# The first stage of a Fourier-mixing and gated-feed-forward kernel in another order

## The chip, the cores and the metric

The kernel runs on one core of a Trainium2 chip. A core has five engines that work side by side, each with its own queue of instructions taken strictly in order: TensorE (matrix products; PE in the profile, its weight loads PEld), VectorE (DVE), ScalarE (ACT), GpSimd (POOL) and SyncE (SP, which here issues the transfers between main memory and the on-chip SBUF). Matrix products land in PSUM, in a few banks that are used in turn. The metric is the time of one execution on the device in microseconds (us), lower is better.

## The reference

For x of 2048 rows and 448 columns, float32 throughout:

```
xn = (x - mean) / sqrt(var + 1e-5)                      # per row
a, b = xn @ hid_re.T, xn @ hid_im.T                     # 448 x 448
s  = seq_re @ a - seq_im @ b                            # 2048 x 2048
g  = silu((gelu(xn @ w_gate) * (xn @ w_up)) @ w_down)   # 448 -> 1792 -> 448
out = x + s * g
```

## The kernel before, in words

**Precision.** To keep float32 accuracy, each operand is split in two: a high part, rounded by a copy to the type `float32r` (mostly on ScalarE), and a low part, the difference of the value and its high part (a subtraction, mostly on VectorE). A product is then three matmuls: high x high, high x low, low x high. In the code these are "hh", "hl" and "lh"; the last, narrow block of the inner dimension goes in "last".

**Tiles.** Rows are dealt in four chunks (`c` = 0 to 3) of four times 128 rows. `xr[c]` holds the raw and then the normalised rows, `xth[c]` and `xtl[c]` the high and low part of the turned (transposed) rows, `xf[c]` a full-precision copy of the first two turned blocks. The inner width 1792 of the feed-forward part is dealt in 14 blocks `f`, in groups of two. For group 0 the two products of gate and up are made plainly (`gu_mm`, `first`, `gateup`); from group 1 on they are made with Strassen's combinations (`strassen`), which take sums and differences of the `xf` blocks of two chunks. `combine(p)` makes these four subtractions for the pair of chunks p, and returns a function that splits one combination into high (`th`) and low (`tl`) part.

**Statistics.** `stats(c, k0, n)` returns four functions: `one(i)` takes mean and variance of 128 rows (two VectorE instructions, L95 and L96), `root` the square root on ScalarE and two short VectorE instructions (L100 to L102), `newton` the reciprocal with a refining step (L106 to L110), `norm(i)` writes the normalised rows (L118). `turn_mm` turns 128 rows on TensorE (four transposes, L127, into one of two PSUM tiles), `turn_split` copies the high part and `xf` on ScalarE (L132, L133) and subtracts the low part on VectorE (L134).

**Weights.** `load_w` brings a block of gate and up weights into one of two `raw` buffers, taken in turn; `prep_w` returns `high` (a copy of 1024 columns, L177 on ScalarE or L179 on VectorE) and `low` (L182 for 768 columns, L184 for 256 columns of half the partitions). `load_d` and `prep_d` do the same for the down weights `wd` (L227 high, L228 low). A `raw` buffer is loaded again when the subtraction that reads it is through.

**Feed-forward.** `act` makes the Gelu of the gate product on ScalarE (L261) and returns `m` (product with the up half, L264, VectorE), `h` (high part, L265, ScalarE) and `l` (low part, L266, VectorE). `down` multiplies them with `wd`: per 128 rows six matmuls into `po` (L286), then a copy into the accumulator `gacc` (L293 on ScalarE for group 0). Between these steps `down` calls what it is handed in `between`.

**Order.** The whole order is written out by hand: under `tc.manual_schedule()` each engine's queue is the order in which the Python code calls it. SyncE issues in the order of the `load_` calls, and transfers share the DMA engines. What an engine waits for follows from the data and from tiles that are used again. The stage at issue is the first: loading, statistics and turning of the four chunks beside group 0 (L378 to L563). In it `first` works on chunk 0 in two halves of 256 columns (rows 0 and 1 of the chunk, then 2 and 3), and later chunks are prepared beside the products of earlier ones. The rest, six groups of Strassen products (L575 to L661), the hidden transform (L683) and the sequence transform (L742 to L764), is the longest part of the time and stays as it is.

Of the kernel before, what the change touches and what calls it, by code (L numbers as in the profile page):

```python
# [8 lines left out]
F32 = mybir.dt.float32  # L9
# [17 lines left out]
GROUPS = [(f, f + 1) for f in range(0, NF, 2)]  # L27
# [3 lines left out]
def fnet_geglu(ctx: ExitStack, tc: tile.TileContext, x, ct, et, wgu, wd, out):  # L31
# [13 lines left out]
    nc = tc.nc  # L45
# [40 lines left out]
    def load_x(c, k0, k1):  # L86
        nc.sync.dma_start(xr[c][:, k0:k1], xv[:, 4 * c + k0 : 4 * c + k1])

    def stats(c, k0, n):
        st = const.tile([P, 4, 6], F32, name=f"st{c}_{k0}", tag="st", bufs=2)  # L90
        mv = const.tile([P, 4, 2], F32, name=f"mv{c}_{k0}", tag="mv", bufs=3)
        sd = const.tile([P, 4, 4], F32, name=f"sd{c}_{k0}", tag="sd", bufs=3)

        def one(i):
            nc.vector.bn_stats(st[:, i], xr[c][:, k0 + i, :D])  # L95
            nc.vector.bn_aggr(mv[:, i], st[:, i])  # L96

        def root():
            r, t, w = sd[:, :n, 0], sd[:, :n, 1], sd[:, :n, 2]
            nc.scalar.activation(t, mv[:, :n, 1], AF.Sqrt, bias=epst)  # L100
            nc.vector.tensor_scalar(w, mv[:, :n, 1], EPS, -0.5, op0=ALU.add, op1=ALU.mult)
            nc.vector.tensor_scalar_mul(sd[:, :n, 3], mv[:, :n, 0], -1.0)  # L102

        def newton():
            r, t, w = sd[:, :n, 0], sd[:, :n, 1], sd[:, :n, 2]
            nc.vector.reciprocal(r, t)  # L106

            nc.vector.tensor_mul(t, r, r)
            nc.vector.tensor_mul(t, t, w)
            nc.vector.scalar_tensor_tensor(r, t, 1.5, r, op0=ALU.add, op1=ALU.mult)  # L110

        def norm(i, eng=nc.vector):
            v = xr[c][:, k0 + i]
            if eng is nc.scalar:
                eng.activation(v, v, AF.Identity, bias=sd[:, i, 3:4])
                eng.activation(v, v, AF.Copy, scale=sd[:, i, 0:1])
            else:
                eng.tensor_scalar(  # L118
                    v, v, mv[:, i, 0:1], sd[:, i, 0:1], op0=ALU.subtract, op1=ALU.mult
                )  # L120

        return one, root, newton, norm
# [7 lines left out]
    def turn_split(c, k, pt):  # L130
        sl = slice(k * P, (k + 1) * P)
        nc.scalar.activation(xth[c][:, :, sl], pt, AF.Copy)  # L132
        nc.scalar.activation(xf[c][:, :, sl], pt[:, :2], AF.Copy)  # L133
        nc.vector.tensor_sub(xtl[c][:, :, sl], pt, xth[c][:, :, sl])  # L134
# [30 lines left out]
    def load_w(f):  # L165
        raw = raw_tile()
        nc.sync.dma_start(raw[:, :1024], wgu[f].rearrange("p b f -> p (b f)"))
        return raw

    def prep_w(slot, raw):  # L170

        w = a_w[:, 2560 * slot : 2560 * slot + 1792]
        wh, wl = w[:, :1024], w[:, 1024:]

        def high(copy):
            if copy is None:
                nc.scalar.activation(wh, raw[:, :1024], AF.Copy)  # L177
            else:
                copy(wh, raw[:, :1024])  # L179

        def low():
            nc.vector.tensor_sub(wl, raw[:, 256:1024], wh[:, 256:])  # L182

            nc.vector.tensor_sub(wh[64:, :256], raw[64:, :256], wh[64:, :256])  # L184

        return high, low, (wh, wl)

# [33 lines left out]
        )  # L221
        return rv

    def prep_d(grp, rv, sub=None):
        o = 1792 * (grp[0] // 2 % 2)
        w = a_d[:, o : o + 1792].rearrange("p (a f d) -> p a f d", a=2, f=2)
        nc.scalar.activation(w[:, 0], rv, AF.Copy)  # L227
        (sub or nc.vector.tensor_sub)(w[:, 1], rv, w[:, 0])  # L228
        return w

    def gu_mm(ps, w, g, c, cols, late_xtl=False):
        hs, ls = zip(*[block(w, k, g) for k in range(4)])
        hh = [(hs[k], xth[c], k) for k in range(3)]
        hl = [(hs[k], xtl[c], k) for k in range(3)]
        lh = [(ls[k], xth[c], k) for k in range(3)]
        last = [(hs[3], xth[c], 3), (hs[3], xtl[c], 3)]
        mm = hh + lh + last[:1] + hl + last[1:] if late_xtl else hh + hl + lh + last
        for n, (a, xt, k) in enumerate(mm):
            nc.tensor.matmul(ps[:, cols], a, xt[:, k, cols], start=n == 0, stop=n == len(mm) - 1)  # L239
# [8 lines left out]
    def hs_tile(name, dt=FR):  # L248
        return sb.tile([P, 2, 512], dt, name=name, tag="hs", bufs=6)
# [7 lines left out]
    def act(f, c, pg):  # L257
        acts[0] += 1
        gt = tmp(acts[0] % 2)
        hs = new_hs(f, c)  # L260
        nc.scalar.activation(gt, pg[0], AF.Gelu_apprx_tanh)  # L261

        return (
            lambda: nc.vector.tensor_mul(gt, gt, pg[1]),  # L264
            lambda: nc.scalar.activation(hs[:, 0], gt, AF.Copy),  # L265
            lambda: nc.vector.tensor_sub(hs[:, 1], gt, hs[:, 0]),  # L266
        )
# [109 lines left out]
    with tc.manual_schedule():  # L377
        load_x(0, 0, 1)  # L378
        load_x(0, 1, 2)
        load_x(0, 2, 4)  # L380
        w_raw = [load_w(0), load_w(1)]
        load_x(1, 0, 4)
        load_x(2, 0, 4)
        load_x(3, 0, 4)
# [50 lines left out]
        xl = [xtl[0][:, :, k * P : (k + 1) * P] for k in range(4)]  # L435
        nc.scalar.activation(xh[0], t0[2], AF.Copy)
        nc.scalar.activation(xh[1], t1[2], AF.Copy)
        one, root, newton, norm = stats(0, 2, 2)
        one(0)
        one(1)  # L440
        ws = [prep_w(i, w_raw[i]) for i in range(2)]
        ws[0][0](nc.vector.tensor_copy)
        nc.vector.tensor_sub(xl[0], t0[2], xh[0])
        nc.vector.tensor_sub(xl[1], t1[2], xh[1])
        root()
        ws[1][0](None)
        for k, t in enumerate((t0, t1)):
            nc.scalar.activation(xf[0][:, :, k * P : (k + 1) * P], t[2][:, :2], AF.Copy)
        ws[0][1]()
        newton()  # L450
        norm(0)
        norm(1)
        ws[1][1]()
        ws = [w[2] for w in ws]
        draw = load_d(GROUPS[0])
        first(0, half[0], ("hh", "hl", "lh", "last"))
# [5 lines left out]
        one(1)  # L462
        turn_split(*t2)
        turn_split(*t3)
        wdn = prep_d(GROUPS[0], draw, nc.gpsimd.tensor_sub)
        one(2)
        one(3)
        root()
# [8 lines left out]
        turn_split(*t0)  # L477
        turn_split(*t1)
        one, root, newton, norm = stats(2, 0, 4)
        one(0)  # L480
        one(1)
        s_raw = load_w(GROUPS[1][0])
        pg = gu_ps(0, 1)
        gu_mm(pg[0], ws[0], 0, 1, half[0], True)
# [1 line left out]
        gu_mm(pg[1], ws[0], 1, 1, half[0])  # L486
        turn_split(*t2)
        turn_split(*t3)
        m0, h0, l0 = act(0, 0, pgs[0])
        m1, h1, l1 = act(1, 0, pgs[1])  # L490
        m0()
        h0()
        l0()
        gu_mm(pg[0], ws[0], 0, 1, half[1], True)
        gu_mm(pg[1], ws[0], 1, 1, half[1])
        m1()
        h1()
        m0, h0, l0 = act(0, 1, pg)
        one(2)
        l1()  # L500
        one(3)
        root()
        m0()
        h0()
        newton()
        for i in range(4):
            norm(i)
        l0()
        pg = gu_ps(1, 1)
        for g in range(2):  # L510
            gu_mm(pg[g], ws[1], g, 1, slice(0, 512))
        one, root, newton, norm = stats(3, 0, 4)
        one(0)
        one(1)
        xf[2] = hs_tile("xf2", F32)
        turn_split(*turn_mm(2, 0))
        down(0, 0, wdn, [lambda k=k: turn_split(*turn_mm(2, k)) for k in (1, 2, 3)])
        m1, h1, l1 = act(1, 1, pg)
        one(2)
        m1()  # L520
        h1()
        one(3)
        l1()
        root()
        newton()
        norm(0)
        norm(1)
# [4 lines left out]
        for c in (2, 3):  # L532
            if c == 2:
                draw = load_d(GROUPS[1])
            else:
                s_raw2 = load_w(GROUPS[1][1])
            m0, h0, l0 = gateup(0, c, ws[0])
            between, between1 = [lambda: (m0(), h0()), l0], []
            if c == 2:
                xf[3] = hs_tile("xf3", F32)  # L540
                turn = lambda k: turn_split(*turn_mm(3, k))
                between = [
                    lambda: (m0(), h0(), norm(2)),
                    lambda: (l0(), norm(3), turn(0)),
                    lambda: turn(1),
                    lambda: turn(2),
                ]
                between1 = [lambda: turn(3)]
            down(0, c - 1, wdn, between)
            if c == 2:  # L550
                nws[0] = prep_s(2, s_raw, nc.vector)
            else:
                one = combine(0)
                for i in range(4):
                    one(i)
                nwdn = prep_d(GROUPS[1], draw)
                late_split = combine(1)
            m1, h1, l1 = gateup(1, c, ws[1], between1)
            m1()
            if c == 2:  # L560
                h1()
                l1()
        late = (h1, l1)  # L563


# [241 lines left out]
```

## Time and profile before

| | before |
|---|---|
| median of 3 runs | 813.77 us (813.35 to 815.39) |
| profiled execution | 814.51 us, of it 812.7 us from the first to the last instruction |
| mean granted TensorE clock | 0.997 |
| TensorE busy | 801.8 us, 99% |
| TensorE weight loads busy | 715.0 us, 88% |
| VectorE busy | 415.0 us, 51% |
| ScalarE busy | 238.7 us, 29% |
| GpSimd busy | 54.4 us, 7% |

The busy times are sums over the execution. VectorE's share differs by stage: it is 7 to 8 tenths in the first third of the span and 2 to 3 tenths in the last part. Matmuls are pipelined, so that the time of one matmul (some 390 ns) is longer than the distance from one to the next. A line number stands for the code line that made the instruction; "issue" stands for time in which an engine waited for nothing that the profile shows.

### The profile page before, as it was taken

Reading aid. Unit: us, or ns where it says so; the run is one execution under the profiler, and the core shown is the slowest. Engines: PE = TensorE matmul, PEld = TensorE weight load, DVE = VectorE, ACT = ScalarE, POOL = GpSimd, SP = SyncE. Lnnn points to the kernel's source line nnn. Section 1 sums busy time; section 2 is a strip of 40 time slices with the busy share of each in tenths; the row PEclk is TensorE's granted clock in tenths of the full one; section 3 lists DMA queues with packets and bytes.
Section 4 is the critical chain, followed back from the end, with each engine's and each line's share of the span. In section 5 each row is a group of like instructions: output and inputs, shape, how many; then the busy total and the mean of one; then the engine's idle time right before and its main releaser. Section 6 shows DMA issues by size and latency. Waiting matters only on the chain.

```text
span 812.7 us, 9386 instructions
## 1 busy us (share of the span) xinstructions
PE 801.8 (99%) x3868; PEld 715.0 (88%) x3868; DVE 415.0 (51%) x626; ACT 238.7 (29%) x356; POOL 54.4 (7%) x62
## 2 busy tenths in 40 slices
PE   8899999999999999999999999999999999999997
PEld 7788888888888888888889999999999999999997
DVE  8776786766776676776763233232232222223221
ACT  3574432322322232232221224122222222222220
POOL 0000120010010010000000000111111111111110
PEclk9999999999999999999999999999999999999999
DMA  8001010000010110100020012344444333444441
GB/s 307 24 0 52 24 52 23 27 27 23 27 49 1 33 43 1 49 23 24 23 77 1 1 38 77 103 140 133 132 127 126 127 127 127 126 127 127 127 127 60
DMA packets 19372, 58.09 MB, mean 71 GB/s; under 512 B 2048, under 2 KB 8064, under 8 KB 18944
## 3 DMA queue, kind: packets, MB, share of 16 engines
q1 hardware_dynamic: 19328, 57.48, 22.1%
q8 instruction: 30, 0.49, 0.2%
q14 instruction: 14, 0.11, 0.0%
HBM read 53.81 MB, written 3.67 MB: 71 GB/s over the span
## 4 chain that ended last, share of the span: by engine, by line
PE 95%; DVE 3%; ACT 1%; issue 1%; DMA 0%; DVEq 0%
PE x L306 22%; PE po L286 16%; PE py L758 13%; PE py L757 13%; PE py L756 13%; PE ab L683 9%; PE x L314 5%; PE gu L239 2%; PE gu L417 1%; PE pt L127 1%; DVE st L95 1%; DVE xr L118 0%; DVE tmp L264 0%; DMA xr<-x 0%; DVE tl L83 0%
## 5 line engine op out<-in xcount | busy, mean ns | idle before, releaser
L286 PE MATMUL po<-wd,hs 128*128 128x448 f32 x672 | 153.0, 366 | 0.0
L286 PEld LDWEIGHTS po<-wd,hs 128*128 128x128 f32 x672 | 125.8, 188 | 14.6 <-ACT gacc L293 0.2
L306 PE MATMUL x<-xt,w 128*128 128x512 f32 x504 | 135.0, 391 | 0.0
L306 PEld LDWEIGHTS x<-xt,w 128*128 128x128 f32 x504 | 94.6, 188 | 17.0
L758 PE MATMUL py<-xt,w 128*128 128x448 f32 x256 | 93.5, 365 | 0.0
L756 PE MATMUL py<-xt,w 128*128 128x448 f32 x256 | 93.5, 365 | 0.0
L757 PE MATMUL py<-xt,w 128*128 128x448 f32 x256 | 93.5, 365 | 0.0
L295 DVE TENSOR_TENSOR gacc<-gacc,po 128x448 f32<-128x448 f32 x96 | 59.3, 618 | 60.8 <-PE po L286 60.8
L306 PE MATMUL x<-th,w 128*128 128x512 f32 x192 | 71.4, 392 | 1.0 <-DVE tmp L264 1.0
L756 PE MATMUL py<-ab,c 128*128 128x448 f32 x192 | 70.1, 365 | 0.0
L757 PE MATMUL py<-ab,c 128*128 128x448 f32 x192 | 70.1, 365 | 0.0
L758 PE MATMUL py<-ab,c 128*128 128x448 f32 x192 | 70.1, 365 | 0.0
L683 PE MATMUL ab<-w,xt 128*128 128x448 f32 x256 | 68.0, 365 | 0.0
L83 DVE TENSOR_TENSOR w<-raw,w 128x1024 fp32r<-128x1024 f32 (+1 forms) x23 | 27.8, 1210 | 73.1 <-ACT w L82 73.1
L82 ACT ACTIVATE w<-raw 128x1024 fp32r<-128x1024 f32 (+1 forms) x23 | 24.2, 1050 | 128.4 <-DMA raw<-ct 118.2
L763 POOL TENSOR_TENSOR gacc<-gacc,s 128x448 f32<-128x448 f32 x15 | 31.0, 2067 | 429.3 <-DVE gacc L762 429.3
L314 PE MATMUL x<-xt,w 128*128 128x512 f32 x192 | 59.2, 389 | 0.0
L762 DVE TENSOR_TENSOR gacc<-gacc,py 128x448 f32<-128x448 f32 (+1 forms) x17 | 10.1, 593 | 87.5 <-PE py L758 87.5
L683 PEld LDWEIGHTS ab<-w,xt 128*128 128x128 f32 x256 | 48.1, 188 | 3.8
L756 PEld LDWEIGHTS py<-xt,w 128*128 128x128 f32 x256 | 48.1, 188 | 3.8
L757 PEld LDWEIGHTS py<-xt,w 128*128 128x128 f32 x256 | 48.1, 188 | 3.8
L758 PEld LDWEIGHTS py<-xt,w 128*128 128x128 f32 x256 | 48.1, 188 | 3.8
(142 smaller groups left out, 1091.1 us busy)
## 6 DMA issues: line engine op xcount, KB each, us to landing
raw<-ct SPq DMA_DIRECT2D x43, 512.0 KB, 4.8
s<-ct SPq DMA_DIRECT2D x21, 512.0 KB, 4.8
raw<-wgu SPq DMA_DIRECT2D x14, 512.0 KB, 3.5
s<-x SPq DMA_DIRECT2D x16, 224.0 KB, 5.2
out<-gacc SPq DMA_DIRECT2D x15, 224.0 KB, 2.0
raw<-wd SPq DMA_DIRECT2D x7, 448.0 KB, 3.3
xr<-x SPq DMA_DIRECT2D x3, 1024.0 KB, 10.9
raw<-et SPq DMA_DIRECT2D x4, 448.0 KB, 3.3
```

What stands on the lines that cost most here:

```text
L82: nc.scalar.activation(h, src, AF.Copy)
L83: nc.vector.tensor_sub(l, src, h)
L239: nc.tensor.matmul(ps[:, cols], a, xt[:, k, cols], start=n == 0, stop=n == len(mm) - 1)
L286: nc.tensor.matmul(po[:, :D], hs[:, a, kk * P : (kk + 1) * P], wdn[:, b, i], start=n == 0, stop=n == 5,)
L295: nc.vector.tensor_add(ga, ga, po[:, :D])
L306: nc.tensor.matmul(ps, a[i], b[j], start=first and n == 0, stop=n == 2, skip_group_check=True)
L314: nc.tensor.matmul(ps, w["k3" + "gu"[g]][0], xt[:, 3], start=False, stop=True, skip_group_check=True)
L683: nc.tensor.matmul(p[:, :D], a, b, start=n == 0, stop=n == len(mm) - 1)
L756: nc.tensor.matmul(py[:, :D], a, h, start=k + r == 0, stop=False)
L757: nc.tensor.matmul(py[:, :D], a, l, start=False, stop=False)
L758: nc.tensor.matmul(py[:, :D], b, h, start=False, stop=q == 3 and i == 7)
L763: (nc.vector if last else nc.gpsimd).tensor_add(ga[:, e], ga[:, e], xres[:, e])
```

## The change

The order of the first stage is changed; the same instructions are made.

- The first load of weights is issued ahead of rows 2 and 3 of chunk 0.
- For chunk 0, the high part of the first weights and their low part come ahead of the second pair of statistics, and the low part (L182, L184) moves from VectorE to GpSimd. The two `one`s stand on both sides of the low parts `xl` of the turned rows.
- The low part of the first `wd` moves from GpSimd to VectorE, and with its high part behind chunk 1's first turned copies, next to `one(0)` of chunk 2.
- The other `one`s of chunk 2, both Gelu products and their parts, and the norms are called in another order. `one(0)` and `one(1)` of chunk 3 move behind the turned copies of chunk 2.
- `combine(0)` with its four splits stood as one piece in front of the last preparation of `wd`. Now the four subtractions come at the end of the step for chunk 2, and the four splits are dealt between the four parts of the following `down`.

```diff
-        def low():
-            nc.vector.tensor_sub(wl, raw[:, 256:1024], wh[:, 256:])
+        def low(eng):
+            eng.tensor_sub(wl, raw[:, 256:1024], wh[:, 256:])
...
-    def prep_d(grp, rv, sub=None):
+    def prep_d(grp, rv, late=False):
...
         nc.scalar.activation(w[:, 0], rv, AF.Copy)
-        (sub or nc.vector.tensor_sub)(w[:, 1], rv, w[:, 0])
+        low = lambda: nc.vector.tensor_sub(w[:, 1], rv, w[:, 0])
+        if late:
+            return w, low
+        low()
         return w
...
         load_x(0, 1, 2)
+        w_raw = [load_w(0)]
         load_x(0, 2, 4)
-        w_raw = [load_w(0), load_w(1)]
+        w_raw.append(load_w(1))
...
+        ws = [prep_w(i, w_raw[i]) for i in range(2)]
+        ws[0][0](nc.vector.tensor_copy)
+        ws[0][1](nc.gpsimd)
         one, root, newton, norm = stats(0, 2, 2)
         one(0)
-        one(1)
-        ws = [prep_w(i, w_raw[i]) for i in range(2)]
-        ws[0][0](nc.vector.tensor_copy)
         nc.vector.tensor_sub(xl[0], t0[2], xh[0])
         nc.vector.tensor_sub(xl[1], t1[2], xh[1])
+        ws[1][0](None)
+        one(1)
         root()
-        ws[1][0](None)
...
-        ws[0][1]()
         newton()
         norm(0)
         norm(1)
-        ws[1][1]()
+        ws[1][1](nc.vector)
...
-        wdn = prep_d(GROUPS[0], draw, nc.gpsimd.tensor_sub)
...
         one, root, newton, norm = stats(2, 0, 4)
+        wdn, d_low = prep_d(GROUPS[0], draw, True)
         one(0)
-        one(1)
+        d_low()
...
         turn_split(*t3)
+        one(1)
         m0, h0, l0 = act(0, 0, pgs[0])
         m1, h1, l1 = act(1, 0, pgs[1])
         m0()
         h0()
+        m1()
+        h1()
+        one(2)
+        one(3)
+        root()
         l0()
+        l1()
+        newton()
+        norm(0)
+        norm(1)
         gu_mm(pg[0], ws[0], 0, 1, half[1], True)
         gu_mm(pg[1], ws[0], 1, 1, half[1])
-        m1()
-        h1()
+        norm(2)
+        norm(3)
         m0, h0, l0 = act(0, 1, pg)
-        one(2)
-        l1()
-        one(3)
-        root()
         m0()
-        h0()
-        newton()
-        for i in range(4):
-            norm(i)
-        l0()
         pg = gu_ps(1, 1)
         for g in range(2):
             gu_mm(pg[g], ws[1], g, 1, slice(0, 512))
+        xf[2] = hs_tile("xf2", F32)
+        turn_split(*turn_mm(2, 0))
+        h0()
+        between = [lambda k=k: turn_split(*turn_mm(2, k)) for k in (1, 2, 3)]
+        turn = between[0]
+        between[0] = lambda: (turn(), l0())
+        down(0, 0, wdn, between)
+        m1, h1, l1 = act(1, 1, pg)
         one, root, newton, norm = stats(3, 0, 4)
         one(0)
         one(1)
-        xf[2] = hs_tile("xf2", F32)
-        turn_split(*turn_mm(2, 0))
-        down(0, 0, wdn, [lambda k=k: turn_split(*turn_mm(2, k)) for k in (1, 2, 3)])
-        m1, h1, l1 = act(1, 1, pg)
-        one(2)
         m1()
         h1()
+        one(2)
         one(3)
+        root()
         l1()
-        root()
...
+            else:
+                between = [
+                    lambda: (m0(), h0(), late_split(0)),
+                    lambda: (l0(), late_split(1)),
+                    lambda: late_split(2),
+                    lambda: late_split(3),
+                ]
             down(0, c - 1, wdn, between)
             if c == 2:
                 nws[0] = prep_s(2, s_raw, nc.vector)
             else:
-                one = combine(0)
-                for i in range(4):
-                    one(i)
                 nwdn = prep_d(GROUPS[1], draw)
                 late_split = combine(1)
...
             if c == 2:
                 h1()
                 l1()
+                late_split = combine(0)
```

More of the change, by code (lines that the diff above doesn't have):

```diff
@@ L179, in high @@
                 copy(wh, raw[:, :1024])
-        def low():
-            nc.vector.tensor_sub(wl, raw[:, 256:1024], wh[:, 256:])
-            nc.vector.tensor_sub(wh[64:, :256], raw[64:, :256], wh[64:, :256])
+        def low(eng):
+            eng.tensor_sub(wl, raw[:, 256:1024], wh[:, 256:])
+            eng.tensor_sub(wh[64:, :256], raw[64:, :256], wh[64:, :256])
         return high, low, (wh, wl)
```

## The prediction

> **What bounds the kernel now.** TensorE is busy for 99% of the span, so only its idle and slow stretches can give time back. I read first who waits for whom on TensorE in the first 110 us, where nearly all of them lie (line, what it waited for, us in total, times, longest):
>
> ```profile
> PE pt L127 <- issue: 3.2, 2, 2.1
> PE x L306 <- DVE tmp L264: 1.0, 1, 1.0
> PE pt L127 <- DVE xt L134: 0.5, 1, 0.5
> PE gu L417 <- DVE w L179: 0.4, 1, 0.4
> ```
>
> The two "issue" waits stand before transposes (L127). Then the chain of work that ended last, over the same stretch (start, us, what):
>
> ```profile
> 4.95 0.31 ACT sd L100
> ...
> 5.28 0.18 DVE sd L106
> ...
> 6.08 1.00 DVE xr L118 x2
> 7.08 0.55 DVE st L95
> ...
> 8.56 0.58 DVE w L179
> ...
> 10.39 0.98 PE gu L417 x6
> 11.39 2.90 PE gu L417 x22
> 14.29 0.87 PE pt L127 x8
> 15.16 5.52 PE gu L417 x44
> 20.69 2.10 issue
> 22.79 1.61 PE pt L127 x8
> 24.40 2.13 PE gu L417 x10
> 26.54 1.38 PE gu L239 x11
> ...
> 30.04 1.28 ACT L261
> ...
> 31.96 0.70 DVE tmp L264
> ...
> 38.38 1.92 DVE xr L118 x4
> ...
> 43.67 1.21 PE po L286 x6
> ...
> 46.55 5.03 PE gu L239 x22
> 51.59 2.43 PE po L286 x12
> ...
> 58.05 2.55 PE gu L239 x11
> ...
> 80.77 0.69 DVE tmp L264
> ```
>
> Up to 10.39 and again up to 22.79 the path runs through VectorE's queue; 22.79 and 39.02 are the transposes of chunks 1 and 2, which wait for normalised rows. Two rows show a second loss: behind the 2.10 us gap eight transposes take 1.61 us (0.87 at 14.29) and ten 256-column matmuls 2.13 us (44 in 5.52 us is 0.1255 each, so 1.26). The view by stretches names the cause (stretch, length, busy time and count of PE, PEld, DVE, ACT, POOL, granted clock, DMA share, GB/s):
>
> ```profile
> 19.90:23.40 3.50, 1.40 (x12) 1.14 (x11) 3.36 (x9) 1.44 (x2) 1.42 (x1) 0.96 0.22 63
> 23.40:26.80 3.40, 3.40 (x18) 3.40 (x18) 2.31 (x6) 1.73 (x4) 0.00 (x0) 0.54 0.19 73
> ```
>
> After the gap the granted clock is 0.54 for 3.4 us. In the first of these stretches VectorE is busy for 3.36 of 3.50 us, but the order of time shows with what:
>
> ```profile
> 10.38 0.95 DVE L182 TENSOR_TENSOR w<-raw,w 128x768 fp32r<-128x768 f32 x1
> 11.37 0.42 DVE L184 TENSOR_TENSOR w<-raw,w 64x256 fp32r<-64x256 f32 x1
> ...
> 19.21 2.11 POOL L228 TENSOR_TENSOR wd<-raw,wd 128x896 fp32r<-128x896 f32 x1 [17.91 <-ACT wd L227]
> ...
> 19.25 2.10 DVE L101 TENSOR_SCALAR sd<-mv 128x4 f32<-128x4 f32 x1
> ...
> 22.14 1.46 DVE L118 TENSOR_SCALAR xr<-xr,mv,sd 128x512 f32<-128x512 f32 x3
> ...
> 39.02 0.63 PE L127 MATMUL pt<-ident,xr 128*128 128x128 f32 x4 [1.15 <-issue]
> ...
> 68.68 0.69 DVE L264 TENSOR_TENSOR tmp<-tmp,gu 128x512 f32<-128x512 f32 x1 [2.89 <-PE gu L239]
> ```
>
> The tiny L101 (four columns) lasts 2.10 us, exactly while GpSimd runs its 2.11 us subtraction L228. That stall stands in the path to the rows that TensorE lacks at 20.69.
>
> **The change, part by part.** All instructions stay; engines, places and one DMA order change. The sum is made against the profiled execution, 814.51 us.
>
> *Weights ahead of rows.* The landings (issue rows of SyncE, then the issues with median us to landing):
>
> ```profile
> 1.63 0.42 SPq L87 DMA_DIRECT2D xr<-x  x1
> 2.10 0.43 SPq L167 DMA_DIRECT2D raw<-wgu  x1
> ```
> ```profile
> xr<-x SPq DMA_DIRECT2D x1, 512.0 KB, 4.4
> raw<-wgu SPq DMA_DIRECT2D x1, 512.0 KB, 6.1
> ```
>
> Today rows 2 and 3 of chunk 0 land at 1.63+4.4 = 6.0, the weights at 2.10+6.1 = 8.2. Both are 512 KB and they are issued next to each other, so I let them swap: weights 6.0, rows 8.2. VectorE finishes its norms at 7.08, copies the weights (0.58) by 7.66 and then stands in `one(0)` until 8.2: 0.54 us of new wait. Behind it in the queue are both `xl` subtractions (L443, L444), which TensorE's second part, "hl", needs. They end at 8.2+0.74+1.21 = 10.15 (0.74 is half of the two `one`s, 7.08 to 8.56; 1.21 from 9.13 to 10.34, the copy's end to just ahead of the 10.39 matmul) against 10.34: 0.14 gained once the hand-over is counted. The 0.4 us wait on the copy L179 goes, but the wait for `xl` takes its place: nothing more.
>
> *Low part of the first weights on GpSimd.* VectorE loses 1.41 us (10.38 to 11.79). Priced from L228 (2.11 for 896 columns) and the 128-column row
>
> ```profile
> L202 POOL TENSOR_TENSOR raw<-raw 128x128 f32<-128x128 f32 x10 | 4.6, 459 | 0.0
> ```
>
> GpSimd pays 0.19 + 2.15 ns a column: 1.84 + 0.74 = 2.6 us, from 7.66 to about 10.3. TensorE needs the first of it when "hl" is through, at 10.25+6x0.1255 = 11.0: covered by 1.4 us. Today that part came late: the 22 matmuls start at 11.39, not at 10.39+0.75, so 0.25 us is gained too. With the 0.14, TensorE reaches the end of its 44 matmuls 0.39 earlier, at 20.30. The cost if the cover fails: L101's row shows that VectorE can stand for as long as GpSimd runs. What runs beside it now is the `one`s and the `xl` subtractions (one input in PSUM); the trace of before has no `one` beside a GpSimd subtraction. Bounds: no effect, as I take it, since what stood beside L228 was a `tensor_scalar` of SBUF operands, another kind of instruction; or VectorE stands from 8.2 until GpSimd ends at 10.3, 2.1 us. The other direction (a gain) is excluded, as GpSimd does nothing here today. Behind the two instructions GpSimd's queue holds nothing until the second group of weights; SyncE's load of wd, which waits for their buffer, goes out 1.5 us earlier (10.3 instead of 11.8), and nothing waits for that. The Trainium skill, "SBUF — State Buffer", section "Who interferes with whom", says that a VectorE instruction with at most one SBUF input outside its two-port modes doesn't contend with GpSimd, while `tensor_scalar` in such a mode does. By that rule only the next L101 is at risk, and the trace agrees in that 2.10 us.
>
> *Low part of wd from GpSimd to VectorE, after `one(0)` of chunk 2.* The 1.94 us stall of L101 (2.10 less the 0.16 that such an instruction takes) leaves the path. The subtraction costs VectorE about 1.1 us (L182's 0.95 scaled from 768 to 896 columns), at a place where it waits for turned rows and Gelus anyway; without that cover, 1.1.
>
> *Chunk 1's rows.* Their norms start at 22.14 now. Less 1.94, less 1.41, plus 0.54 for the rows of chunk 0, plus twice about 0.17 for a root on ScalarE that those two covered (from 4.95 to L106 at 5.28 is 0.33, two short VectorE instructions hide half): 19.67. The transposes follow 0.65 later (22.14 to 22.79): 20.32, and TensorE arrives at 20.30. So they start 2.45 us earlier, and the gap is gone: 2.45.
>
> *Clock.* Without the gap, 22.79 to 26.54 (3.75) becomes 0.87+1.26 = 2.13: 1.62. The Trainium skill, "TensorE: Matmul & The Clock Gate", section "Why this matters for your kernels", sets the limit for such gaps at some 3 us; here 2.1 us was followed by the slow stretch, so I go by the trace. By the page's limit this gap would be innocent and the 1.62 would stay, a rival below.
>
> *Chunk 2.* From 26.54 to 39.02 are 12.48 us; the content is 44 matmuls (5.52), eight transposes (0.87) and 22 of 512 columns (5.03): 11.42, so 1.06 are lost, and TensorE would now arrive at 39.02-2.45-1.62-1.06 = 33.9. Are the rows there? Shifted by 4.07, the table load starts at 25.97 and the first Gelu product at 27.9. The new VectorE queue from there: two products (1.2), `one(2)`, `one(3)` (1.48), two short ones (0.2), two low parts (1.3), newton (0.80, 5.28 to 6.08): 32.9, plus 0.65 gives 33.5. Just in time; today the third product stood ahead of the norms at 38.38. 1.06 gained.
>
> *Turning chunk 2 beside `down`.* 39.02 to 46.55 is 7.53; the content is 4 x (0.44+1.21) = 6.60. The 0.93 came from transposes that waited for a subtraction L134 behind two `one`s (0.5 in the waits) and from `po` copies behind them. `one(0)`, `one(1)` of chunk 3 now come after the turned copies: 0.93. *Next chunk:* 51.59 to 58.05 is 6.46, the content 2.43+3x0.44+2x1.21 = 6.17: 0.29.
>
> *Combinations in two places.* Four subtractions (some 0.69 each, as row 80.77) plus four splits stood ahead of the last Gelu product, for which a matmul waited 1.0 us. The first four move to where VectorE sits idle for 2.89 us (68.68). That frees 2.8 us; the splits stay tied to `po` copies on ScalarE, and I leave half, 1.4, against 1.0 needed: 1.0.
>
> Sum: 2.45+1.62+1.06+0.93+0.29+1.0 = 7.35, giving 807.2 for that execution and 806.4 against the median, which is 0.74 lower. At three places the margin is under 0.5 us, which the rows can't resolve; I give back 0.2 for each: 807.0.
>
> **The rivals.**
> A. GpSimd holds up VectorE at the start (first bound above): 2.1 us late in a queue that ends at TensorE, so 807.0+2.1 = 809.1. For it: L101's row. Against it: a different kind of instruction stood.
> B. The half-rate stretch has another cause than the gap and stays: 808.6. For it: the page's limit. Against it: matmuls before and after run at full clock, and it follows the only 2 us gap.
> C. The second half gives its gain back: chunk 2's norms now sit behind both products and both low parts; if ScalarE's order (two copies, then two table loads of 1.28) makes them late, 1.06+0.93+0.29 go, 809.3, and at worst part of the first gain waits there again, up to 812.
> D, on the other side. VectorE stands in `one(0)` for the rows of chunk 0, ahead of everything. Each us that they land after 8.2 costs one. It decides at 8.2+6.8 = 15.0 us; if they landed at 17, say, the time would be 807.0+8.8 = 815.8. For it: the weights in that place took 6.1 us for bytes that the neighbour had in 4.4. Against it: these two landed in the order of their issue.
>
> **How the numbers follow.** Forecast 0.70, A 0.08, B 0.06, C 0.10 (0.03 of it within 0.3%), D 0.06 (0.02 of it within 0.3%, 0.04 beyond). A change under 0.3% (2.4 us) can't be told from none here. Faster is 0.70+0.08+0.06+0.07 = 0.91, same 0.05, slower 0.04. The low end is every wait closed, 806.4, less 0.8 for the scatter (the three runs lie 2 us apart); the high end takes in A, B and the middle of C: 805.6 to 809.7.
>
> **What would show it.** Right: no "issue" wait of 2 us ahead of a transpose, a granted clock of 1.00 all through 20 to 30 us, L101 never over 0.3 us, first "hl" matmul near 10.25, first product wait of L306 gone, gateup of chunk 2 starting near 40.5 rather than 46.55. Wrong: `one(0)` ends much after 9, a long L95 or L101 beside L182 on GpSimd, another slow-clock stretch, or a new idle before chunk 2's transposes near 34 us.

## The result and the profile after

The changed kernel takes 809.31 us (median of 4 runs, 807.68 to 809.93) against 813.93 us before (4 runs, the three of the table above and one more, 813.35 to 815.39): a ratio of 0.9937, 95% interval 0.9917 to 0.9958. By the medians it is faster by 4.6 us, inside the range, and by less than the 6.8 us of the forecast. The profiled execution took 809.93 us, 4.58 less than that of before; the sum had promised 7.35.

Who waits for whom on TensorE in the first 110 us, after the change (line, what it waited for, us in total, times, longest):

```profile
PE gu L421 <- DVE xt L448: 2.1, 1, 2.1
PE warm L403 <- DVE junk L393: 1.5, 1, 1.5
PE pt L127 <- issue: 0.2, 1, 0.2
```

The waits before the transposes of chunks 1 and 2 (3.2 us) are gone; the 0.2 us that is left stands at 7.00, before those of chunk 0. The waits on L134 and on the last Gelu product are gone too. (L403 is the warm-up before the first data; its 1.5 us stood there before as well.) But the "hl" matmuls wait 2.1 us for the second `xl` subtraction (now L448). Before, the same wait was short:

```profile
PE gu L417 <- DVE xt L444: 0.2, 1, 0.2
```

The chain of work that ended last shows where the new wait comes from:

```profile
2.11 7.63 DMA xr<-x
...
9.77 0.64 DVE st L95
...
10.61 0.57 DVE xt L447
11.19 0.61 DVE xt L448
...
11.84 5.10 PE gu L421 x28
16.94 0.87 PE pt L127 x8
17.81 5.34 PE gu L421 x44
23.15 1.07 PE pt L127 x8
24.22 1.19 PE gu L421 x10
...
43.52 5.06 PE gu L242 x22
48.57 2.43 PE po L289 x12
...
54.76 2.54 PE gu L242 x11
```

From 11.84 on the chain, as far as 110 us, is TensorE at work; before, it was interrupted three times after the first "hl" matmul (ahead of 22.79, of 43.02 and of 81.50). But it begins with a load: the rows, issued at 2.11, land 7.63 us later, and VectorE stands for them. In order of time:

```profile
7.99 0.69 DVE L179 CAST w<-raw 128x1024 fp32r<-128x1024 f32 x1 [0.63 <-DMA raw<-wgu]
...
8.77 1.82 POOL L182 TENSOR_TENSOR w<-raw,w 128x768 fp32r<-128x768 f32 x1 [7.46 <-DVE w L179]
...
9.77 0.63 DVE L95 BATCH_NORM_STATS2 st<-xr 128x6 f32<-128x448 f32 x1 [1.09 <-DMA xr<-x]
...
10.67 0.72 POOL L184 TENSOR_TENSOR w<-raw,w 64x256 fp32r<-64x256 f32 x1
...
21.29 0.17 DVE L101 TENSOR_SCALAR sd<-mv 128x4 f32<-128x4 f32 x1
```

The weights land at 7.96 and the rows at 9.74, where the prediction had 6.0 and 8.2. L101 is back to 0.17 us. And the slow clock has moved: it is no longer behind chunk 1's rows, but behind the new wait (columns as in the prediction's view by stretches, the granted clock third from the end):

```profile
13.00:16.50 3.50, 3.50 (x21) 3.50 (x21) 3.30 (x9) 0.41 (x2) 0.00 (x0) 0.62 0.94 388
16.50:20.00 3.50, 3.50 (x31) 3.48 (x30) 2.66 (x7) 1.64 (x4) 0.00 (x0) 1.00 0.63 189
```

Twenty-eight matmuls that take 3.51 us at full clock (0.1255 each) took 5.10.

### The profile page after: what moved, and what is told of

Same layout as the page of the kernel before. It is cut to its first block, busy times and chain, and to the rows that moved or that the text cites. A ratio compares the mean times of both kernels' runs of the same rounds, so it can differ in the third digit from the quotient of the medians.

```text
span 808.2 us, 9388 instructions
## 1 busy us (share of the span) xinstructions
PE 800.2 (99%) x3868; PEld 714.7 (88%) x3868; DVE 413.5 (51%) x625; ACT 238.3 (29%) x356; POOL 54.9 (7%) x63
## 4 chain that ended last, share of the span: by engine, by line
PE 98%; DMA 1%; DVE 0%; SPq 0%; issue 0%
PE x L309 22%; PE po L289 17%; PE py L770 13%; PE py L771 13%; PE py L772 13%; PE ab L697 9%; PE x L317 5%; PE gu L242 4%; PE gu L421 1%; DMA xr<-x 1%; PE pt L127 1%; SPq L87 0%; DVE gacc L777 0%; DVE gacc L776 0%; DVE st L95 0%; DVE xt L448 0%
```

## The experiments

They ran in three sets, each on one chip with its own runs of the kernel before (medians 814.81, 814.28 and 814.09). The ratios to before, with 95% intervals, can be compared across sets.

| kernel | set | median, us | ratio to before |
|---|---|---|---|
| changed kernel again | 1 | 808.45 | 0.9926 (0.9913 to 0.9938) |
| rows first | 1 | 808.61 | 0.9930 (0.9917 to 0.9943) |
| xl first | 1 | 807.84 | 0.9917 (0.9903 to 0.9930) |
| data order | 1 | 808.56 | 0.9925 (0.9912 to 0.9937) |
| combinations as before | 2 | 810.38 | 0.9950 (0.9938 to 0.9963) |
| wd alone | 2 | 812.34 | 0.9978 (0.9969 to 0.9986) |
| start as before | 2 | 809.40 | 0.9936 (0.9923 to 0.9949) |
| chunk 2 as before | 2 | 811.16 | 0.9966 (0.9954 to 0.9978) |
| rows last | 3 | 811.26 | 0.9964 (0.9952 to 0.9976) |
| loads held | 3 | 808.32 | 0.9924 (0.9911 to 0.9937) |
| xl first, loads held | 3 | 807.61 | 0.9919 (0.9908 to 0.9931) |
| both low parts on GpSimd | 3 | 807.85 | 0.9926 (0.9914 to 0.9937) |

One thing bears on all of these times. The slow stretch comes in some executions of a kernel and not in others. In the fourteen profiles the mean granted clock is 0.998 or less where there is such a stretch in the first 45 us, and 0.999 or more where there is none. By that mark 18 of the 37 executions of the kernel before in the three sets had one; their median is 815.17 us, against 814.04 for the other 19.

**The changed kernel again.** No edit.

> The changed kernel once more, as the yardstick of this set. Landing theory: rows 2 and 3 of chunk 0 land some 7.6 us after their issue (9.74 in the profile shown), VectorE stands in the first L95 for about 1.1 us, TensorE waits about 2.1 us for xl (L448) and then runs 3.4 us at a low clock: 809.3 us. Chance theory: that profile caught an unlucky landing; this one shows the rows at about 8.2, a wait of xl under 0.5 us and no slow stretch, and the time is nearer 807.

The rows landed at 2.10 + 7.2 = 9.3 and TensorE's wait was 1.4 us, so the late landing is not peculiar to one profile. The slow stretch is less constant: this execution had none (granted clock 1.00 from 9 to 22.4 us), and it took 808.45.

```profile
PE gu L421 <- DVE xt L448: 1.4, 1, 1.4
PE pt L127 <- issue: 0.4, 1, 0.4
```

**Rows first.** The changed kernel with the old order of loads:

```diff
-        w_raw = [load_w(0)]
         load_x(0, 2, 4)
-        w_raw.append(load_w(1))
+        w_raw = [load_w(0), load_w(1)]
```

> The changed kernel with the old order of loads (rows 2 and 3 of chunk 0 ahead of the first weights), all else as changed. Landing theory: rows at about 6.0, weights at 8.2; now the copy L179 stands for about 0.5 us, one(0) ends at 9.5, xl at 10.75, the wait of TensorE for L448 shrinks from 2.1 to about 1.0 us, and chunk 1's transposes start near 21.1 instead of 23.1: 1.5 to 2.5 us faster than the changed kernel, about 807. Port theory (VectorE is slowed by the subtraction on GpSimd beside it): the wait stays at 2 us and the time at 809.

The wait for `xl` fell to 0.9 us, but 0.6 came up on the copy of the weights, which landed at 2.10 + 6.5 = 8.6; chunk 1's transposes started at 21.61, the time is the same (808.61). About 807 was expected; that missed. The order of the two loads as such is worth nothing that the runs show: here the weights, now second, held VectorE's queue in the place of the rows.

**Data order.** Old order of loads, and VectorE's queue as `one(0)`, copy, both `xl`, `one(1)`:

```diff
...
+        one, root, newton, norm = stats(0, 2, 2)
+        one(0)
         ws = [prep_w(i, w_raw[i]) for i in range(2)]
         ws[0][0](nc.vector.tensor_copy)
         ws[0][1](nc.gpsimd)
-        one, root, newton, norm = stats(0, 2, 2)
-        one(0)
         nc.vector.tensor_sub(xl[0], t0[2], xh[0])
         nc.vector.tensor_sub(xl[1], t1[2], xh[1])
+        one(1)
         ws[1][0](None)
-        one(1)
```

> The changed kernel with the old order of loads and the queue of VectorE in the order in which the data land: one(0), copy of the weights, low part on GpSimd, both xl, one(1). Landing theory: VectorE never stands for a load except some 0.4 us before the copy, xl ends near 10.0, TensorE's wait for L448 is under 0.5 us, chunk 1's transposes start near 20.3, no slow stretch: 2 to 3 us faster than the changed kernel, about 806.5 to 807. Port theory: about 809.

A miss: 808.56, no gain. In this profile the rows, in front, landed 6.3 us after their issue and the weights 7.1 (9.2), so the wait stood before the copy, 1.3 us.

**xl first.** The new order of loads, but nothing that TensorE needs stands behind the rows:

```diff
-        one(0)
         nc.vector.tensor_sub(xl[0], t0[2], xh[0])
         nc.vector.tensor_sub(xl[1], t1[2], xh[1])
+        one(0)
```

> The changed kernel with both xl subtractions ahead of one(0), new order of loads. Landing theory: xl ends at about 9.9 whatever the rows do, TensorE's wait for L448 falls from 2.1 to about 0.3 us; but the statistics still wait for the rows at 9.74, so chunk 1's transposes come only about 1 us earlier, and up to 2 us of idle stand before them instead (with a slow clock behind, if it is long enough): between 807.5 and 809.5. If the rows are not what holds the start, the wait for L448 stays at about 2 us.

TensorE's wait for `xl` is gone, and its first 34 matmuls run in one piece:

```profile
8.65 4.82 PE L421 MATMUL gu<-xt,w 128*128 128x256 f32 x34
13.31 1.04 PE L127 MATMUL pt<-ident,xr 128*128 128x128 f32 x8
14.35 2.89 PE L421 MATMUL gu<-xt,w 128*128 128x256 f32 x22
17.60 2.89 PE L421 MATMUL gu<-xt,w 128*128 128x256 f32 x22 [0.36 <-DVE xt L134]
20.86 1.13 PE L127 MATMUL pt<-ident,xr 128*128 128x128 f32 x8 [0.37 <-issue]
```

Small waits of 0.4 take its place, not the 2 us that I had thought possible; chunk 1's transposes start at 20.86 instead of 21.67. The median is 0.6 us under the changed kernel's in the same set; the intervals overlap, so the runs don't prove it faster. No execution of it met a slow stretch (clock 0.999 or 1.000 in all five).

**Rows last.** The suspected cause doubled: rows behind both loads of weights.

```diff
-        w_raw = [load_w(0)]
+        w_raw = [load_w(0), load_w(1)]
         load_x(0, 2, 4)
-        w_raw.append(load_w(1))
```

> The changed kernel with rows 2 and 3 of chunk 0 behind both loads of weights: the cause doubled. Landing theory: the rows land 0.8 to 1.5 us later still (10 to 11), VectorE stands about 2 us in the first L95, and TensorE's wait for L448 grows from 1.4 to 2.1 to 2.5 to 3.5 us, with the slow clock behind it in most runs: 1 to 2 us slower than the changed kernel, near 810. If the rows are not the cause, the wait stays at 2 us or less and the time at 808.5 to 809.3.

```profile
10.76 0.63 DVE L95 BATCH_NORM_STATS2 st<-xr 128x6 f32<-128x448 f32 x1 [2.11 <-DMA xr<-x]
```
```profile
PE gu L420 <- DVE xt L447: 3.0, 1, 3.0
```

The rows landed at 10.74, 1.0 to 1.4 us later than in the two profiles of the changed kernel. VectorE stood 2.1 us, TensorE waited 3.0, and the ratio rose from 0.9926 to 0.9964, about 3 us more, beyond the 1 to 2 us that were expected: late rows in front of `xl` are the cause of the wait. The mean clock was 0.996 to 0.998 in all five executions, so the slow stretch was always there, and its cost is in the 3 us.

**Loads held.** The 1 MB loads of chunks 2 and 3 issued behind the load of wd, once in the changed kernel alone and once together with the edit of "xl first":

```diff
-        load_x(2, 0, 4)
-        load_x(3, 0, 4)
...
         draw = load_d(GROUPS[0])
+        load_x(2, 0, 4)
+        load_x(3, 0, 4)
```

Alone:

> The changed kernel with the 1 MB loads of chunks 2 and 3 issued later, behind the load of wd. It tells why the rows land late. If transfers share the DMA engines, rows and weights of chunk 0 land earlier (rows at 8 or before, weights at 6.5) and the wait for L448 shrinks by 1 us. If each transfer waits only for those issued ahead of it, nothing changes: rows at 9.3 to 9.7, wait 1.4 to 2.1 us, 808.5 to 809.3.

With "xl first":

> xl first together with the held loads of chunks 2 and 3; candidate for the fastest. If transfers share: weights land about 1 us earlier than 7.8, everything from there 0.5 to 1 us earlier, 807.0. If not: as xl first alone, 807.8.

Inconclusive on why they land late. Alone: weights 6.8 us after their issue, rows 7.7, later than without; together with xl first: 4.3 and 5.8, the earliest of all. Such a split came without the edit too. All fourteen profiles side by side (us from issue to landing; third and fourth load of the queue, both 512 KB, issued at about 1.64 and 2.10):

| profile | third load | lands after | fourth load | lands after |
|---|---|---|---|---|
| before | rows | 4.4 | weights | 6.1 |
| rows first | rows | 4.7 | weights | 6.5 |
| data order | rows | 6.3 | weights | 7.1 |
| start as before | rows | 6.3 | weights | 7.1 |
| wd alone | rows | 6.8 | weights | 7.6 |
| changed | weights | 6.3 | rows | 7.6 |
| changed, again | weights | 6.1 | rows | 7.2 |
| xl first | weights | 6.1 | rows | 7.0 |
| both low parts | weights | 6.1 | rows | 6.9 |
| combinations as before | weights | 6.6 | rows | 7.4 |
| chunk 2 as before | weights | 6.6 | rows | 7.4 |
| rows last | weights | 6.3 | weights | 7.1 |
| loads held | weights | 6.8 | rows | 7.7 |
| xl first, loads held | weights | 4.3 | rows | 5.8 |

The place in the queue sets the landing, not what is loaded: rows and weights are alike. But a third load lands after 4.3 to 4.7 us in three profiles, and after 6.1 to 6.8 in eleven. The profile of before was one of the three. What makes the difference stays open, but one thing can be read from the profiles. The loads up to the third one make 1.05 MB. When the third had landed, the core had moved 1.34 to 1.41 MB in all in the three early profiles and 1.74 to 2.20 MB in the eleven late ones, at no lower mean rate (216 to 237 GB/s from the start of the span, against 220 to 264). So the late case is not a slower transfer: more bytes of loads issued behind the third were moved ahead of its last ones. That was so with the loads held too (1.95 MB at 8.44 us), with only three more loads issued by then.

**wd alone.** The kernel before, with only the low part of wd on VectorE, behind `one(0)` of chunk 2:

```diff
-        wdn = prep_d(GROUPS[0], draw, nc.gpsimd.tensor_sub)
...
+        wdn, d_low = prep_d(GROUPS[0], draw, True)
         one(0)
+        d_low()
         one(1)
```

> The kernel before with one part of the change alone: the low part of the first wd on VectorE, behind one(0) of chunk 2. Forecast's theory: L101 lasts 0.2 instead of 2.1 us, chunk 1's transposes start near 20.9 instead of 22.8, and the low-clock stretch behind the gap is gone: 2 us and up to 1.6 more, near 810.5 to 812 where before runs at 814. Rival (clock has another cause): 1.9 us and a low-clock stretch as before, 812.5. If L101 still lasts 2 us, GpSimd was not what held it.

L101 lasts 0.17 us, and in this profile the weights land late:

```profile
10.73 0.95 PE L420 MATMUL gu<-xt,w 128*128 128x256 f32 x6 [1.74 <-DVE w L179]
```
```profile
21.20 0.17 DVE L101 TENSOR_SCALAR sd<-mv 128x4 f32<-128x4 f32 x1
```

So GpSimd held L101. The gap before chunk 1's transposes is closed: 1.6 us of "issue" waits are left of 3.2, of which 1.1 stand before chunk 2. In this profile TensorE's own lateness has a part in that: after the 1.74 us wait and a slow stretch from 11.7 to 15.1 it is through with its 44 matmuls at 23.0, where before it was at 20.69. The ratio is 0.9978, by the medians 1.9 us against the 1.94 us stall, a third or so of the change. The median of 812.34 misses the 810.5 to 812 that was expected and lies by the 812.5 of the rival. But the rival's slow stretch didn't stay: one of these eleven executions has a mean clock below 0.999, the profiled one, against eight of 17 of the kernel before in this set. The expectation had counted the stretch as if every execution had it. Among executions without it the difference is 1.75 us (814.07 to 812.32).

**Combinations as before.** The changed kernel with `combine(0)` and its splits in one piece again (the hunks of the change undone).

> The changed kernel with combine(0) and its four splits as one piece in the old place. Forecast's theory: the last Gelu product comes 1.4 us or more later again and a matmul waits for it, as in the kernel before (1.0 us at L306): 1.0 us slower than the changed kernel, which ran at 808.45 in the last set; so near 809.5. Rival: the wait came from the general lateness of VectorE in the old first stage, and is gone with that; no wait, no difference.

```profile
78.01 0.50 PE L309 MATMUL x<-th,w 128*128 128x512 f32 x1 [1.01 <-DVE tmp L267]
```

The 1.01 us came back to the hundredth. The median is 1.1 us above the changed kernel's first (809.31) and the ratio is 0.0013 to 0.0024 above its two. The runs also show what the clock is worth: in three executions with a mean clock of 0.997 this kernel took 810.96 to 811.09, in the other three (0.999 to 1.000) 808.71 to 809.79. As only three of the changed kernel's nine executions show the slow stretch, the times bear out the size of the 1.0 us loosely; the profile shows it.

**Chunk 2 as before.** The changed kernel with the old order from chunk 2's statistics to chunk 3's; wd's low part stays on VectorE.

> The changed kernel with the old order from chunk 2's statistics to chunk 3's (wd's low part stays on VectorE). Forecast's theory: the idle before chunk 2's transposes (1.15), the waits while they are turned beside the down products (0.93) and of the next chunk (0.29) come back: 2.3 us slower than the changed kernel, near 810.7. Rival: with an earlier chunk 1 the old order has slack enough, and less than 1 us comes back.

```profile
36.84 0.63 PE L127 MATMUL pt<-ident,xr 128*128 128x128 f32 x4 [1.11 <-issue]
...
40.84 0.66 PE L127 MATMUL pt<-ident,xr 128*128 128x128 f32 x4 [0.48 <-DVE xt L134]
```

Both waits are back at their old length, and the ratio is 0.9966 against 0.9926 to 0.9937: 2.4 to 3.3 us, where 2.3 was expected. The rival (slack enough) falls.

**Start as before.** The changed kernel with its start for chunk 0 undone: old order of loads, both `one`s ahead, low part of the first weights on VectorE ahead of `newton`.

```diff
...
+        one, root, newton, norm = stats(0, 2, 2)
+        one(0)
+        one(1)
         ws = [prep_w(i, w_raw[i]) for i in range(2)]
         ws[0][0](nc.vector.tensor_copy)
-        ws[0][1](nc.gpsimd)
-        one, root, newton, norm = stats(0, 2, 2)
-        one(0)
         nc.vector.tensor_sub(xl[0], t0[2], xh[0])
         nc.vector.tensor_sub(xl[1], t1[2], xh[1])
+        root()
         ws[1][0](None)
-        one(1)
-        root()
...
+        ws[0][1](nc.vector)
         newton()
```

> The changed kernel with its start for chunk 0 undone: old order of loads, both statistics ahead, low part of the first weights on VectorE. Forecast's theory: VectorE carries 1.41 us more ahead of chunk 1's rows, chunk 1's transposes start 0.9 to 1.4 us later than in the changed kernel's second profile (21.67): about 1.3 us slower, near 809.7. Landing theory: the new order of loads costs about what the move to GpSimd saves, and the time is within 0.5 us of the changed kernel's 808.45.

Its ratio, 0.9936, lies between the changed kernel's two results: the whole rearrangement of chunk 0 brings between nothing and 0.8 us, not the 1.3 that was expected. TensorE's "hl" starts at 11.34 in its profile, at 11.84 and 11.37 in the changed kernel's. The late landing strikes the old start as well: here TensorE waits 1.5 us for the copy of the weights (L179).

**Both low parts on GpSimd.** xl first, and the second weights' low part on GpSimd too:

```diff
         ws[1][0](None)
+        ws[1][1](nc.gpsimd)
         one(1)
...
-        ws[1][1](nc.vector)
```

> xl first, and the low part of the second weights on GpSimd as well, right behind its high part. Without contention VectorE has 1.4 us less ahead of chunk 1's rows, whose transposes start 0.4 us earlier (TensorE's own work then sets them): 807.4. Port theory: GpSimd runs from about 11.4 to 14.0, beside newton and both norms L118 of rows 2 and 3 (tensor_scalar of SBUF operands); as L101 did in the kernel before, they stand until it is through, up to 2.5 us each way; then chunk 0's transposes come late and TensorE waits ahead of them: 808.5 to 810.

```profile
11.52 1.82 DVE L101 TENSOR_SCALAR sd<-mv 128x2 f32<-128x2 f32 x1
...
13.52 0.62 DVE L108 TENSOR_TENSOR sd<-sd 128x2 f32<-128x2 f32 x1
```
```profile
11.47 1.84 POOL L182 TENSOR_TENSOR w<-raw,w 128x768 fp32r<-128x768 f32 x1 [0.27 <-POOL w L184]
13.39 0.72 POOL L184 TENSOR_TENSOR w<-raw,w 64x256 fp32r<-64x256 f32 x1
```
```profile
PE pt L127 <- DVE xr L118: 1.7, 1, 1.7
```

The contention is there: a two-column `tensor_scalar` takes 1.82 us beside 1.84 of GpSimd, and a two-column `tensor_tensor` with two SBUF inputs 0.62 instead of 0.16. TensorE waits 1.7 us for the norms. Yet the time is 807.85, neither the 807.4 nor the 808.5 to 810 that were expected; the 1.4 us that VectorE is spared ahead of chunk 1 may pay for it, which was not tried apart.

## Why the prediction was right, and where it was not

*The step that failed is the landing: "I let them swap: weights 6.0, rows 8.2".* The swap by place holds, the times did not: I took one profile's landings, 4.4 and 6.1 us after issue, as fixed, and they are the early case. In the late case, the common one, the weights ahead of the rows land 6.1 to 6.8 us after their issue and the rows 6.9 to 7.7. So, in the profiled execution, `one(0)` stood until 9.74, `xl` ended at 11.79 instead of 10.15 and "hl" began at 11.84 instead of 10.25: 1.59 us. This is rival D's place and price, with a landing 1.5 us late instead of 7. Two of the signs that the prediction named for being wrong came: `one(0)` ended at 10.61, and there was another slow stretch. As the late landing comes with the old start too, part of what the sum missed is that it set a profile with an early landing against one with a late one.

*The clock* was right in its cause, and wrong in that it would stay full. It was also counted too high for the median: the 1.62 us stand in an execution that has the slow stretch, and by the mean clock half the executions of before had none. The gap at 20.69 is gone, and with it the slow stretch there; the wait at 9.8 to 11.8 made a new one, and 28 matmuls cost 1.59 more. Together 3.18; transposes of chunk 1 start at 23.15 in the chain where the sum had 20.32, 2.83 later, close to the 2.77 by which the profiled executions miss the sum. In the second profile of the changed kernel, without the slow stretch, they start at 21.67, still 1.35 later than in the sum. Rival B falls: the slow stretch went with the gap and came with another, and no profile has one without such an idle ahead of it (last section).

*Low part on GpSimd.* Priced right: 1.82 and 0.72 against 1.84 and 0.74. Rival A falls: L95 beside L182 took 0.63, as ever, and the copy of the weights and GpSimd's work stand in line anyway. "Both low parts" shows that the risk was real one step further on, at L101; in the changed kernel GpSimd is through at 11.4 and L101 comes at 12.57. The Trainium skill, "SBUF — State Buffer", "Who interferes with whom", names just these kinds (`tensor_scalar` in a two-port mode, `tensor_tensor` with two SBUF inputs) and excludes an instruction with at most one SBUF input outside such modes; all three agree with the runs (1.82, 0.62 and 0.63). The prediction had taken only L101 to be at risk; L108 is too.

*wd's low part*: right, 1.94 forecast, 1.75 to 1.9 measured alone.

*Chunk 2, turning, next chunk*: right. From chunk 1's transposes to the products of chunk 2 the chain now takes 43.52-23.15 = 20.37 us, 0.87+1.26+11.42+6.60 = 20.15 was the content; the next `down` takes 54.76-48.57 = 6.19 against 6.17. Undone, 2.4 to 3.3 came back for 2.28. Rival C falls.

*Combinations*: right, 1.0 forecast, 1.01 in the profile when undone.

Small slips in the sum change nothing: 22.79 - 20.32 is 2.47 and not 2.45, the `xl` subtractions gain 0.19 and not 0.14 (the hand-over stands on both sides), and GpSimd's first part is ready 1.5 us ahead of its use, not 1.4.

So the gain is some 1.9 from wd, 2.4 to 3.3 from chunk 2, 1.0 from the combinations, and next to nothing from the start: 5.3 to 6.2 by the parts, between the 4.6 us of the first comparison and the 6.4 of the second (814.81 to 808.45). How many executions meet a slow stretch is in each of these times and was not separated.

## What to carry to other kernels

One profile shows one draw of the first loads' landing times; before an order is built on them, look at several profiles, and put behind a late load only what nobody waits for (here: `xl` ahead of the statistics, which ended that wait and the slow stretch behind it, though the runs don't prove the kernel faster). A VectorE instruction of two columns can cost as much as a whole subtraction on GpSimd, so ask what stands beside GpSimd's work, not how small it is. An idle TensorE is paid twice where the slow clock follows, so shortening an idle stretch below the border given in the next section is worth more than its length.

## What the runs showed that I had not expected

The landing of equal loads in the same place of the queue falls into two groups, 4.3 to 4.7 and 6.1 to 6.8 us, with nothing in the kernel that tells them apart.

The clock falls after idle stretches well under 3 us. The trace's record of the granted clock changes only at steps of 3.41 us, counted from a point that differs between executions. TensorE's idle times within one such step added up to 2.99, 2.10, 2.06, 1.74, 1.71 and 1.64 us in six profiles (rows last, before, changed, wd alone, combinations as before, start as before), and the next step ran at half clock. With 1.58 and 1.44 us (chunk 2 as before, data order) it did not. Nor did it where a wait of 1.4, 1.6 or 1.7 us lay across two steps (changed again, loads held, both low parts), so that no step held more than 1.32. Two profiles with the same wait show how close this is, "combinations as before" first:

```profile
11.63 5.11 PE L421 MATMUL gu<-xt,w 128*128 128x256 f32 x28 [1.58 <-DVE xt L448]
```
```profile
11.60 3.62 PE L421 MATMUL gu<-xt,w 128*128 128x256 f32 x28 [1.58 <-DVE xt L448]
```

In the first, another 0.13 us of idle, ahead of the products that start at 9.11, fell in the same step. So in these profiles the border lies between 1.58 and 1.64 us within a step, and chance decides by where the steps fall. The Trainium skill, "TensorE: Matmul & The Clock Gate", section "Part 1: The HAM clock gate (the "warmup" mystery)", describes the free-running window of 3413 ns, which these records show. The Trainium skill's advice on that page, section "Why this matters for your kernels", to avoid gaps above about 3 us is too generous here.
